# Native-unit softmax normalisation and the first layer's w_out low parts: which engine does them

## The chip, the cores and the metric

The kernel runs on one core of one Trainium2 chip. The metric is the time of one execution on the device in microseconds (us); what is compared is the median of several runs. The core's engines work side by side, each through its own instruction queue in a fixed order: TensorE (PE in the profile; PEld is its weight load), VectorE (DVE), ScalarE (ACT), GpSimd (POOL) and SyncE (SP, which issues DMAs here).

## What is computed

A causal attention with a forget bias, then two MLPs. Shapes: q, k, v are 4 x 8 x 576 x 64 (batch, heads, positions, head width); the MLPs take 2304 tokens of width 512 through 2048 hidden channels. The weights come as float64.

```
scores = where(causal, -1e9, scale * q @ k.T + min(bias, 0))
attn = exp(scores - max(scores))
attn = attn / (sum(attn) + 1e-9)
x = (attn @ v), heads side by side: 2304 x 512
x = (s * max(x @ moe_w_in, 0) ** 2 + b) @ moe_w_out
h = x @ moe2_w_in
out = (max(h, 0) + alpha * min(h, 0)) @ moe2_w_out
```

## The kernel before

**Attention in units.** A unit is one batch, one range of query rows (rows 0 to 319 in three blocks, or rows 320 to 575 in two) and one pair of heads: 32 units in all. The first eight, all of batch 0, are called *native*: their matmuls run on plain float32. The first four of these run before any MLP work. The other 24 split each operand into a high and a low float32r part.

**A head of a unit** (`scores`, then `values`) goes through the engines like this. The bias goes into a tile `probs` (VectorE L435 for head 0, ScalarE L431 for head 1), GpSimd masks its diagonal (L439), TensorE makes the scores (L457), VectorE adds both and takes the running maximum (L461), ScalarE takes the exponential and its row sum (L473). VectorE adds 1e-9 and takes the reciprocal of the sums (L480, L481), the blocks are multiplied by it (L484), TensorE transposes them (L515), a copy brings them out of PSUM (L519, ScalarE or VectorE) and TensorE multiplies them by v (L531). A block is 64 x 64, 128 x 192 or 128 x 320 elements in the first range, 128 x 448 or 128 x 576 in the second.

**Weights in packets.** The first layer's 16 packets each hold a w_in and a w_out tile of 128 x 512. Each tile is loaded as float64, made into float32 by three instructions (`convert`: ScalarE L140, VectorE L141 and L142) and then split: ScalarE casts the high part (L130), and the low part is the difference of the tile and its high part (L131, helper `split`). All 16 packets are made while the native units run.

**MLP blocks.** A block is 256 tokens; at each of 16 steps it takes one packet up (L783) and down (L897). Its hidden tile is split too, in the first layer by ScalarE (`gh`) and GpSimd (`gl`, L131). The first MLP block needs units 0 to 3; the next ones need later units, which are interleaved with the running block.

**The order.** The code gives a program order, and a scheduler lays out each engine's queue from it. At the start of attention, dummy matmuls (L97) are placed at fixed points among the first four units' work.

Of the kernel before, what the change touches and what calls it, by code (L numbers as in the profile page):

```python
# [12 lines left out]
AF = mybir.ActivationFunctionType  # L13
ALU = mybir.AluOpType
# [5 lines left out]
def tile_forget_attention__then__two_mlps(  # L20
# [20 lines left out]
    nc = tc.nc  # L41
# [52 lines left out]
    def busy(n):  # L94

        for _ in range(n):
            tc.keep_in_program_order(nc.tensor.matmul(scratch, dense[:, :P], dense, start=True, stop=True))  # L97
# [31 lines left out]
    def split(hi, lo, src, lo_eng=nc.vector):  # L129
        nc.scalar.copy(hi, src)  # L130
        lo_eng.tensor_tensor(out=lo, in0=src, in1=hi.bitcast(F32), op=ALU.subtract)  # L131
# [14 lines left out]
    def slot(n, dtype, name):  # L146
        return wp.tile([P, 512], dtype, tag=f"w{n}", name=name)
# [27 lines left out]
    def weight_tiles(f):  # L175

        if f not in SPARE:
            return [slot(n, F32R, f"w1_{f}_{n}") for n in SPLIT[SLOT[f]]]
        tiles = []
        for tag, pool, cols, n in SPARE[f]:  # L180
            t = pool.tile([P, cols], F32R, tag=tag, name=f"w1_{f}_{len(tiles)}")
            tiles += [t[:, i * 512 : (i + 1) * 512] for i in range(n)]
            if f == 0:
                rests.append(t[:, 512 : 512 + 2 * P])
        return tiles
# [3 lines left out]
    def fetch(layer, f):  # L189
        if (layer, f) in fetched:  # L190
            return fetched[layer, f]
        w_in, w_out = ((w_in1, w_out1), (w_in2, w_out2))[layer]


        def raw(name, n):
            if layer == 1:
                if f % 2:
                    tile_ = one.tile([P, 1024], U32, tag=("xh0", "xl0")[n], name=name)
                else:
                    tile_ = two.tile([P, 1088], U32, tag="probs", name=name)  # L200
            else:
                pool, tag = RAW[2 * f + n]
                tile_ = pool.tile([P, 20 * D if tag == "vs" else 1024], U32, tag=tag, name=name)
            return tile_[:, :1024].rearrange("p (n z) -> p n z", z=2)

        wi = raw(f"wi{layer}_{f}", 0)
        wo = raw(f"wo{layer}_{f}", 1)
        nc.sync.dma_start(
            out=wi.rearrange("p (c n) z -> p c (n z)", c=NCC),
            in_=w_in[:, f * 2 * P : (f + 1) * 2 * P].rearrange("(c p) n -> p c n", p=P),  # L210
        )
        nc.sync.dma_start(out=wo.rearrange("p n z -> p (n z)"), in_=w_out[f * P : (f + 1) * P, :])
        fetched[layer, f] = wi, wo
        return wi, wo

    def load_packet(layer, f):
        wi, wo = fetch(layer, f)
        t = weight_tiles(f) if layer == 1 else []
        values_ = []
        for n, src in enumerate((wi, wo)):  # L220
            if layer == 1:
                pool, tag, cols = WT[(2 * f + n) % len(WT)]
                wt = pool.tile([P, cols], U32, tag=tag, name=f"wt{f}_{n}")[:, :512]
            elif (f, n) == (NF - 1, 1):
                wt = two.tile([P, 512], U32, tag="ph", name="last")
            else:
                wt = slot(WHOLE[f][n], U32, f"wt0_{f}_{n}")
            convert(src, wt)
            values_.append(wt.bitcast(F32))
        for n, wt in enumerate(values_):  # L230
            if layer == 0:
                t += [slot(m, F32R, f"w0_{f}_{len(t)}_{m}") for m in SPLIT[f][2 * n : 2 * n + 2]]
            split(t[2 * n], t[2 * n + 1], wt, nc.gpsimd if layer == 0 and n else nc.vector)
        return [x.rearrange("p (c n) -> p c n", c=NCC) for x in t[:2]] + t[2:]


# [167 lines left out]
    def scores(u, h):  # L404

        own = HALF[h]
        head = u.b * H + u.h0 + h
        flip = u.native and h == 1
        nr = len(u.blocks)
        nm = two.tile([P, 3], F32, tag="nm", name=f"nm_{u.tag}_{h}")  # L410
        sm = two.tile([P, 3], F32, tag="sm", name=f"sm_{u.tag}_{h}")
        if u.rng == 0:
            nc.gpsimd.memset(sm[:, 0:1], 1.0)
        big = None if u.early else two.tile([P, 1088], F32, tag="probs", name=f"probs_{u.tag}_{h}")
        probs, col = {}, 0
        for r in u.blocks:
            i0, i1 = IB[r]
            rows = i1 - i0
            if u.early and r != 1:
                big, col = u.buf(two, 0, F32, "", f"probs{h}{r}"), 0  # L420

            width = -(-i1 // P) * P if i1 < S else S
            pt = probs[r] = big[:, col : col + width]
            col += width
            if width > i1:
                nc.gpsimd.memset(pt[:, i1:], 0.0)
            if r == 0:
                nc.gpsimd.memset(pt[64:P, 0:64], 0.0)

            if flip:  # L430
                nc.scalar.activation(  # L431
                    pt[:rows, :i1], u.cums[h][:rows, :i1], AF.Relu, scale=-1.0, bias=cumT[:rows, r, head : head + 1]
                )
            else:
                nc.vector.tensor_scalar(  # L435
                    out=pt[:rows, :i1], in0=u.cums[h][:rows, :i1], scalar1=cumT[:rows, r, head : head + 1],
                    scalar2=0.0, op0=ALU.subtract, op1=ALU.min,
                )
            nc.gpsimd.affine_select(  # L439
                out=pt[:rows, i0:i1], in_=pt[:rows, i0:i1], pattern=[[-1, rows]], base=0,  # L440
                channel_multiplier=1, compare_op=ALU.is_ge,
                fill=-MASKED if flip else MASKED,
            )
        u.probs[h] = probs
        for m, r in enumerate(u.blocks):
            i0, i1 = IB[r]
            rows, n = i1 - i0, i1
            a0 = i0 - u.q0
            pt = probs[r]
            init = -KEEP_ALL if flip else KEEP_ALL  # L450
            for j0, j1 in ([(0, n)] if n <= 512 else [(0, 320), (320, n)]):
                sc = u.bank("sc", f"sc{h}_{r}_{j0}")

                scr, all_ = sc[:rows, : j1 - j0], sc[:, : j1 - j0]
                aq = slice(a0, a0 + P)
                if u.native:
                    nc.tensor.matmul(all_, u.qk[0][own, aq], u.qk[1][own, j0:j1], start=True, stop=True)  # L457
                else:
                    nc.tensor.matmul(all_, u.xs[h][0][:, aq], u.xs[h][1][:, j0:j1], start=True, stop=False)
                    nc.tensor.matmul(all_, u.ql[h][:, aq], u.xs[h][1][:, j0:j1], start=False, stop=True)  # L460
                nc.vector.tensor_tensor_reduce(  # L461
                    out=pt[:rows, j0:j1], in0=scr, in1=pt[:rows, j0:j1], scale=SCALE if flip else -SCALE, scalar=init,
                    op0=ALU.subtract if flip else ALU.add, op1=ALU.max if flip else ALU.min,
                    accum_out=nm[:rows, m : m + 1],
                )
                if u.n < EARLY:
                    busy(1)
                init = nm[:rows, m : m + 1]
            if flip:
                nc.vector.tensor_scalar(  # L470
                    out=nm[:rows, m : m + 1], in0=nm[:rows, m : m + 1], scalar1=-1.0, scalar2=None, op0=ALU.mult
                )
            nc.scalar.activation(  # L473
                pt[:rows, :n], pt[:rows, :n], AF.Exp, bias=nm[:rows, m : m + 1], scale=1.0 if flip else -1.0,
                accum_out=sm[:rows, m : m + 1],
            )
            yield
        if u.n == 0:
            busy(4)
        nc.vector.tensor_scalar(out=sm[:, :nr], in0=sm[:, :nr], scalar1=1e-9, scalar2=None, op0=ALU.add)  # L480
        nc.vector.reciprocal(sm[:, :nr], sm[:, :nr])  # L481
        for m, r in enumerate(u.blocks):
            rows, n = IB[r][1] - IB[r][0], IB[r][1]
            nc.gpsimd.tensor_scalar(  # L484
                out=probs[r][:rows, :n], in0=probs[r][:rows, :n], scalar1=sm[:rows, m : m + 1],
                scalar2=1.0, op0=ALU.mult, op1=ALU.mult,
            )
        yield

    def values(u, h):  # L490
# [465 lines left out]
    def packet(layer, f):  # L956
        if (layer, f) not in packets:
            packets[layer, f] = load_packet(layer, f)
        return packets[layer, f]
# [92 lines left out]
```

## Time and profile before

| | us |
|---|---|
| runs shown: median (lowest to highest) | 1039.78 (1039.27 to 1041.05) |
| profiled execution, its own time | 1040.97 |
| span from its first to its last instruction | 1039.2 |
| TensorE busy in the span | 1019.4 |
| VectorE, ScalarE, GpSimd busy | 681.3, 672.4, 457.6 |

The profiled execution took 1.77 us beside its span and 1.19 us more than the median. TensorE's busy time is a union of overlapping matmuls whose ends are modelled, so a busy TensorE can still be waiting now and then. Shares over the whole span hide that the first 135 us differ from the rest: attention of the native units and the making of the packets lie there.

### The profile page before, as it was taken

Reading aid. Unit: us, or ns where it says so; the run is one execution under the profiler, and the core shown is the slowest. Engines: PE = TensorE matmul, PEld = TensorE weight load, DVE = VectorE, ACT = ScalarE, POOL = GpSimd, SP = SyncE. Lnnn points to the kernel's source line nnn. Section 1 sums busy time; section 2 is a strip of 40 time slices with the busy share of each in tenths; the row PEclk is TensorE's granted clock in tenths of the full one; section 3 lists DMA queues with packets and bytes.
Section 4 is the critical chain, followed back from the end, with each engine's and each line's share of the span. In section 5 each row is a group of like instructions: output and inputs, shape, how many; then the busy total and the mean of one; then the engine's idle time right before and its main releaser. Section 6 shows DMA issues by size and latency. Waiting matters only on the chain. (4 is left out here: it accounts for less than half of the span.)

```text
span 1039.2 us, 20636 instructions
## 1 busy us (share of the span) xinstructions
PE 1019.4 (98%) x6952; PEld 925.8 (89%) x6952; DVE 681.3 (66%) x1605; ACT 672.4 (65%) x1669; POOL 457.6 (44%) x876
## 2 busy tenths in 40 slices
PE   9899999999999999999999999999999999999997
PEld 4568899999999999999999888888899999999996
DVE  6979865787676776677655865857665456455443
ACT  5877876777787877778776776645454455445433
POOL 5656775666677666777562000574611011001000
PEclk9999999999999999999999999999999999999999
DMA  7988433343232432334215762645644335334331
GB/s 167 255 211 239 132 68 70 71 93 79 40 92 64 102 72 52 79 68 91 66 35 173 240 192 74 207 147 170 196 163 142 103 112 172 103 99 136 104 104 46
DMA packets 197930, 125.45 MB, mean 121 GB/s; under 512 B 138496, under 2 KB 167936, under 8 KB 197824
## 3 DMA queue, kind: packets, MB, share of 16 engines
q1 hardware_dynamic: 193744, 123.56, 42.8%
q8 instruction: 55, 0.90, 0.4%
q10 hardware_dynamic: 4080, 0.57, 0.3%
q14 instruction: 51, 0.42, 0.1%
HBM read 106.19 MB, written 17.90 MB: 119 GB/s over the span
## 5 line engine op out<-in xcount | busy, mean ns | idle before, releaser
L783 PE MATMUL hp<-xh,w 128*128 128x256 f32 (+1 forms) x1024 | 229.0, 300 | 0.3 <-ACT r L802 0.3
L907 PE MATMUL acc<-w,ring 128*128 128x512 f32 x864 | 214.6, 392 | 1.1 <-DVE ring L131 0.7
L907 PEld LDWEIGHTS acc<-w,ring 128*128 128x128 f32 x864 | 155.8, 188 | 29.3 <-DVE ring L131 1.1
L783 PEld LDWEIGHTS hp<-xh,w 128*128 128x128 f32 x1024 | 171.4, 189 | 6.2 <-ACT r L802 0.5
L897 PE MATMUL acc<-gh,w 128*128 128x256 f32 x896 | 172.4, 286 | 0.5 <-ACT res L926 0.5
L783 PE MATMUL hp<-xl,w 128*128 128x256 f32 (+1 forms) x512 | 152.6, 298 | 0.0
L897 PEld LDWEIGHTS acc<-gh,w 128*128 128x128 f32 x896 | 136.0, 189 | 3.2 <-issue 1.6
L883 POOL TENSOR_TENSOR cc<-u,t 128x256 f32<-128x256 f32 x32 | 26.1, 817 | 235.5 <-DVE u L874 201.5
L897 PE MATMUL acc<-gl,w 128*128 128x256 f32 x448 | 118.7, 288 | 2.2 <-POOL gl L131 2.2
L484 POOL TENSOR_SCALAR probs<-probs,sm 64x64 f32<-64x64 f32 (+4 forms) x160 | 91.0, 581 | 60.5 <-DVE sm L481 49.9
L473 ACT ACTIVATE probs<-probs,nm 64x64 f32<-64x64 f32 (+4 forms) x160 | 90.0, 563 | 38.5 <-DVE nm L461 32.7
L131 POOL TENSOR_TENSOR gl<-r,gh 128x256 fp32r<-128x256 f32 x112 | 89.5, 799 | 48.6 <-ACT gh L130 42.1
L817 PE MATMUL p<-xs,sums 128*128 128x256 f32 x768 | 104.7, 282 | 0.4 <-DVE u L859 0.4
L783 PEld LDWEIGHTS hp<-xl,w 128*128 128x128 f32 x512 | 97.1, 190 | 3.3 <-issue 0.4
L817 PEld LDWEIGHTS p<-xs,sums 128*128 128x128 f32 x768 | 98.0, 189 | 2.1 <-DVE u L859 0.6
L461 DVE CUSTOM_DVE_ANT_0 probs<-sc,probs 128x320 f32<-128x320 f32 (+3 forms) x160 | 68.2, 427 | 41.2 <-PE sc L460 32.8
L817 PEld LDWEIGHTS p<-xs,w 128*128 128x128 f32 x576 | 79.0, 189 | 8.7 <-DVE u L874 2.0
L802 ACT ACTIVATE r<-hp 128x256 f32<-128x256 f32 (+1 forms) x144 | 58.0, 403 | 44.1 <-PE hp L783 33.2
L817 PE MATMUL p<-xs,w 128*128 128x256 f32 x576 | 82.3, 282 | 2.4 <-DVE u L874 1.5
L897 PEld LDWEIGHTS acc<-gl,w 128*128 128x128 f32 x448 | 80.1, 188 | 5.0 <-POOL gl L131 2.8
L828 DVE SCALAR_TENSOR_TENSOR ph<-pl,misc,ph 128x512 f32<-128x512 f32 x64 | 51.7, 807 | 42.4 <-ACT pl L844 42.4
L515 PE MATMUL pt<-ident,probs 128*128 128x128 f32 x480 | 74.3, 275 | 4.6 <-POOL probs L484 4.4
(149 smaller groups left out, 2116.8 us busy)
## 6 DMA issues: line engine op xcount, KB each, us to landing
sums<-sums_d SPq DMA_DIRECT2D x128, 256.0 KB, 2.7
wi<-in_moe_w_in_dram SPq DMA_DIRECT2D x32, 512.0 KB, 4.7
wo<-in_moe_w_out_dram SPq DMA_DIRECT2D x32, 512.0 KB, 4.8
cum<-cum_d SPq DMA_DIRECT2D x32, 288.0 KB, 3.7
sums_d<-w SPq DMA_DIRECT2D x64, 128.0 KB, 1.8
cum<-cum_d SPq DMA_DIRECT2D x30, 160.0 KB, 3.0
nat<-in_k_dram SPq DMA_DIRECT2D x64, 72.0 KB, 2.5
x_d<-res SPq DMA_DIRECT2D x18, 256.0 KB, 2.2
```

What stands on the lines that cost most here:

```text
L131: lo_eng.tensor_tensor(out=lo, in0=src, in1=hi.bitcast(F32), op=ALU.subtract)
L461: nc.vector.tensor_tensor_reduce(out=pt[:rows, j0:j1], in0=scr, in1=pt[:rows, j0:j1], scale=SCALE if flip else -SCALE, scalar=init, op0=AL ...
L473: nc.scalar.activation(pt[:rows, :n], pt[:rows, :n], AF.Exp, bias=nm[:rows, m : m + 1], scale=1.0 if flip else -1.0, accum_out=sm[:rows, m ...
L484: nc.gpsimd.tensor_scalar(out=probs[r][:rows, :n], in0=probs[r][:rows, :n], scalar1=sm[:rows, m : m + 1], scalar2=1.0, op0=ALU.mult, op1=A ...
L515: nc.tensor.transpose(tp[:, o : o + P], u.probs[h][r][:, k0 : k0 + P], ident)
L783: nc.tensor.matmul(hs, a[:, c], b[c], start=(n == 0), stop=(n == len(terms) * NCC - 1))
L802: relus.append(nc.scalar.activation(r, hs, AF.Relu, scale=1.0 / W_SCALE).ins)
L817: nc.tensor.matmul(bank, lhs[:, c * P : (c + 1) * P], rhs[:, c], start=(start and c == 0 and z == 0), stop=(c == 1 and z == 2), skip_group ...
L828: nc.vector.scalar_tensor_tensor(out=r, in0=u, scalar=nalpha[:, f : f + 1], in1=r, op0=ALU.mult, op1=ALU.add).ins
L883: nc.gpsimd.tensor_tensor(out=cc[:, T:], in0=u3, in1=t5, op=ALU.add)
L897: nc.tensor.matmul(banks[d] if count == 2 else acc[d // 2][:, d % 2], a[:, d * P : (d + 1) * P], b, start=(f == 0 and (d % 2 == 0 or count ...
L907: nc.tensor.matmul(banks[m], a[:, m * P : (m + 1) * P], b, start=(f == 0 and b is woh and a is gh), stop=(f == NF - 1 and a is gl),)
```

## The change

Two pieces of work leave GpSimd. The 20 multiplications of head 0 of the eight native units (4 units with 3 blocks, 4 with 2) go to ScalarE, as a Copy with a scale per row; the 20 of head 1 go to VectorE. The 24 other units keep GpSimd. And the low parts of the first layer's 16 w_out tiles go from GpSimd to VectorE, which makes those of w_in already. From the line of the edit on, line numbers of the changed kernel are 3 to 6 higher.

```diff
@@ load_packet
-            split(t[2 * n], t[2 * n + 1], wt, nc.gpsimd if layer == 0 and n else nc.vector)
+            split(t[2 * n], t[2 * n + 1], wt, nc.vector)
@@ scores
         for m, r in enumerate(u.blocks):
             rows, n = IB[r][1] - IB[r][0], IB[r][1]
-            nc.gpsimd.tensor_scalar(
-                out=probs[r][:rows, :n], in0=probs[r][:rows, :n], scalar1=sm[:rows, m : m + 1],
-                scalar2=1.0, op0=ALU.mult, op1=ALU.mult,
-            )
+            pt, by = probs[r][:rows, :n], sm[:rows, m : m + 1]
+            if not u.native:
+                nc.gpsimd.tensor_scalar(out=pt, in0=pt, scalar1=by, scalar2=1.0, op0=ALU.mult, op1=ALU.mult)
+            elif h:
+                nc.vector.tensor_scalar(out=pt, in0=pt, scalar1=by, scalar2=None, op0=ALU.mult)
+            else:
+                nc.scalar.activation(pt, pt, AF.Copy, scale=by)
         yield
```

The scheduler lays the queues out anew. The first place is VectorE's queue at head 1 of the first unit, before (-) and now (+). Here `sm` holds the sums, `probs_0_0_1_333` is the head's tile, and `wt_0_0_196` the first weight tile.

```order
 L481 RECIPROCAL sm_0_0_1_331<-sm_0_0_1_331 128x3
 L470 TENSOR_SCALAR nm_1_0_1_442<-nm_1_0_1_442 64x1
-L461 ISA probs_0_1_0_445,nm_1_0_1_442<-sc_1_0_0_1_0_478,probs_0_1_0_445 128x192
-L461 ISA nm_1_0_1_442 128x1
+L470 TENSOR_SCALAR nm_1_0_1_442<-nm_1_0_1_442 128x1
+L488 TENSOR_SCALAR probs_0_0_1_333<-probs_0_0_1_333,sm_0_0_1_331 64x64
+L488 TENSOR_SCALAR probs_0_0_1_333<-probs_0_0_1_333,sm_0_0_1_331 128x192
+L488 TENSOR_SCALAR probs_0_0_1_333<-probs_0_0_1_333,sm_0_0_1_331 128x320
+L375 STREAM_TRANSPOSE turnedq_3_0_377<-natq_3_0_179 128x320
+L141 TENSOR_SCALAR wt_0_0_196<-wt_0_0_196 128x512
+L375 STREAM_TRANSPOSE turnedk_3_0_378<-natk_3_0_180 128x320
 L480 TENSOR_SCALAR sm_1_0_0_382<-sm_1_0_0_382 128x3
```

The three multiplications now stand right behind the reciprocal, and the first weight tile's conversion (L141) stands behind them.

The second place is GpSimd's queue between the units 2 and 4; first before, where `w0_1_2`, `w0_2_2` and `w0_3_2` are low parts of w_out tiles of packets 1 to 3:

```order
L131 TENSOR_TENSOR w0_1_2_5_239<-wt0_1_1_230,w0_1_2_6_238 128x512
L484 TENSOR_SCALAR probs10_0_2_0_585<-probs10_0_2_0_585,sm_0_2_0_1_583 64x64
L484 TENSOR_SCALAR probs10_0_2_0_585<-probs10_0_2_0_585,sm_0_2_0_1_583 128x192
L484 TENSOR_SCALAR probs12_0_2_0_597<-probs12_0_2_0_597,sm_0_2_0_1_583 128x320
L413 MEMSET sm_0_3_0_1_723 128x1
L484 TENSOR_SCALAR probs00_0_3_0_664<-probs00_0_3_0_664,sm_0_3_0_0_662 64x64
L131 TENSOR_TENSOR w0_2_2_9_259<-wt0_2_1_250,w0_2_2_10_258 128x512
L484 TENSOR_SCALAR probs00_0_3_0_664<-probs00_0_3_0_664,sm_0_3_0_0_662 128x192
L484 TENSOR_SCALAR probs02_0_3_0_676<-probs02_0_3_0_676,sm_0_3_0_0_662 128x320
L131 TENSOR_TENSOR w0_3_2_13_658<-wt0_3_1_649,w0_3_2_14_657 128x512
```

And now:

```order
L413 MEMSET sm_0_2_0_1_583 128x1
L413 MEMSET sm_0_3_0_0_662 128x1
L439 AFFINE_SELECT probs_0_0_1_0_817<-probs_0_0_1_0_817 128x128 x2
L439 AFFINE_SELECT probs_0_0_1_1_923<-probs_0_0_1_1_923 128x128 x2
L413 MEMSET sm_0_3_0_1_723 128x1
L426 MEMSET probs_0_1_1_0_987 128x64
L439 AFFINE_SELECT probs_0_1_1_0_987<-probs_0_1_1_0_987 128x128 x2
L131 TENSOR_TENSOR gl0_0_0_895<-r0_0_896,gh0_0_0_894 128x256
```

Only masks, small memsets and then the low parts `gl` of the first MLP block are left there.

The third place is TensorE's queue at the transposes (`pt0_0_0_1_1`) of head 0 of unit 5; `hp0_0_n` is the up step n of the first MLP block. First before:

```order
L897 MATMUL acc0_0_1_880<-gh0_0_1_1179,w0_1_2_5_239 128x256
L515 MATMUL pt0_0_0_1_1_1062<-ident_85,probs_0_1_1_0_987 128x128
L457 MATMUL sc1_4_0_0_1_1_1069<-turned_0_1_1_863 128x320
L457 MATMUL sc1_4_320_0_1_1_1072<-turned_0_1_1_863 128x256
L515 MATMUL pt0_0_0_1_1_1062<-ident_85,probs_0_1_1_0_987 128x128 x3
L515 MATMUL pt0_1_0_1_1_1079<-ident_85,probs_0_1_1_0_987 128x128 x5
L783 MATMUL hp0_0_3_1258<-xh0_0_869,w0_3_0_12_653 128x256
```

And now:

```order
L900 MATMUL acc0_0_1_880<-gl0_0_3_1272,w0_3_2_14_657 128x256
L518 MATMUL pt0_0_0_1_1_1062<-ident_85,probs_0_1_1_0_987 128x128
L457 MATMUL sc1_4_0_0_1_1_1069<-turned_0_1_1_863 128x320
L457 MATMUL sc1_4_320_0_1_1_1072<-turned_0_1_1_863 128x256
L518 MATMUL pt0_0_0_1_1_1062<-ident_85,probs_0_1_1_0_987 128x128 x3
L518 MATMUL pt0_1_0_1_1_1079<-ident_85,probs_0_1_1_0_987 128x128 x5
L786 MATMUL hp0_0_6_1536<-xh0_0_869,w0_6_0_24_1234 128x256
```

The MLP's up steps 3 to 5, the rest of its down step 1 and its down steps 2 and 3 now stand ahead of these transposes. From unit 9 on the two orders of TensorE differ only by a few swapped neighbours, and beyond the first third of each queue all of them read alike.

## Rows read from the trace of the kernel before

**Rows 1.** Busy time in four stretches; counts, clock, DMA share.

```profile
core 0: us, PE busy (x) PEld busy (x) DVE busy (x) ACT busy (x) POOL busy (x), PEclk, DMA share, GB/s
0.00:62.00 62.00, 55.52 (x227) 30.85 (x228) 48.27 (x159) 40.91 (x116) 35.95 (x112) 0.94 0.87 213
29.50:50.00 20.50, 18.59 (x82) 11.61 (x83) 19.53 (x68) 19.30 (x56) 10.98 (x24) 0.92 0.94 238
62.00:135.00 73.00, 71.80 (x473) 60.73 (x472) 65.81 (x133) 59.56 (x142) 48.52 (x70) 1.00 0.69 181
300.00:400.00 100.00, 100.00 (x837) 99.79 (x836) 71.34 (x209) 78.98 (x212) 68.15 (x143) 1.00 0.33 76
```

**Rows 2.** Waits of TensorE's weight loads, 0 to 62 us: total, times, longest.

```profile
PEld pt L515 <- POOL probs L484: 6.4, 8, 3.2
```

**Rows 3.** GpSimd's groups, 0 to 130 us: busy, mean ns, idle before.

```profile
L484 POOL TENSOR_SCALAR probs<-probs,sm 64x64 f32<-64x64 f32 (+4 forms) x38 | 24.0, 644 | 21.6 <-DVE sm L481 11.7 <-ACT xf L546 5.3 <-DVE nm L470 4.5
L131 POOL TENSOR_TENSOR w<-wt,w 128x512 fp32r<-128x512 f32 x15 | 19.9, 1328 | 9.7 <-ACT w L130 4.9 <-DVE w L131 3.2 <-ACT wt L140 1.5
```

**Rows 4.** VectorE's weight groups, forms apart, 0 to 140 us.

```profile
L141 DVE TENSOR_SCALAR wt<-wt 128x512 uint32<-128x512 uint32 x31 | 20.2, 656 | 3.3 <-ACT wt L140 3.1
L142 DVE SCALAR_TENSOR_TENSOR wt<-wi,wt 128x512 uint32<-128x512 uint32 x16 | 16.0, 997 | 0.2
L142 DVE SCALAR_TENSOR_TENSOR wt<-wo,wt 128x512 uint32<-128x512 uint32 x15 | 12.3, 821 | 0.1
```

**Rows 5.** Single lines, 0 to 140 us: ns min/median/max.

```profile
L141 DVE TENSOR_SCALAR wt<-wt x31: 385/506/1582, 19.5 to 124.3; 128x512 uint32<-128x512 uint32 x31
L142 DVE SCALAR_TENSOR_TENSOR wt<-wi,wt x16: 673/852/1776, 19.9 to 124.7; 128x512 uint32<-128x512 uint32 x16
L142 DVE SCALAR_TENSOR_TENSOR wt<-wo,wt x15: 668/682/1652, 25.0 to 122.9; 128x512 uint32<-128x512 uint32 x15
L131 DVE TENSOR_TENSOR w<-wt,w x16: 644/682/1242, 25.6 to 127.6; 128x512 fp32r<-128x512 f32 x16
```

**Rows 6.** VectorE in order of time: start us, us.

```profile
44.40 1.65 DVE L142 SCALAR_TENSOR_TENSOR wt<-wo,wt 128x512 uint32<-128x512 uint32 x1
...
49.37 1.88 DVE L435 TENSOR_SCALAR probs<-cum,cumT 128x448 f32<-128x448 f32 x2
```

**Rows 7.** GpSimd in order of time, beside these.

```profile
44.09 1.26 POOL L131 TENSOR_TENSOR w<-wt,w 128x512 fp32r<-128x512 f32 x1
45.34 1.70 POOL L484 TENSOR_SCALAR probs<-probs,sm 128x192 f32<-128x192 f32 x2
...
49.59 1.33 POOL L131 TENSOR_TENSOR w<-wt,w 128x512 fp32r<-128x512 f32 x1 [2.55 <-DVE w L131]
...
52.69 1.52 POOL L484 TENSOR_SCALAR probs<-probs,sm 64x64 f32<-64x64 f32 x3
```

**Rows 8.** VectorE's bias pair of a later unit, in order of time.

```profile
65.44 0.86 DVE L435 TENSOR_SCALAR probs<-cum,cumT 128x448 f32<-128x448 f32 x2
```

**Rows 9.** Bias groups of the native units, 0 to 130 us.

```profile
L431 ACT ACTIVATE probs<-cum,cumT 128x448 f32<-128x448 f32 (+4 forms) x17 | 8.8, 575 | 0.4 <-DMA cum<-cum_d 0.3
L435 DVE TENSOR_SCALAR probs<-cum,cumT 128x448 f32<-128x448 f32 (+4 forms) x17 | 11.2, 704 | 0.0
```

**Rows 10.** The end of unit 3's head 1: VectorE, then TensorE, in order of time.

```profile
52.36 0.16 DVE L481 RECIPROCAL sm<-sm 128x3 f32<-128x3 f32 x1
...
53.76 0.55 PE L515 MATMUL pt<-ident,probs 128*128 128x128 f32 x3 [2.79 <-POOL probs L484]
```

**Rows 11.** A wait of TensorE's weight loads, 62 to 135 us.

```profile
PEld acc L897 <- POOL gl L131: 1.0, 1, 1.0
```

**Rows 12.** First up matmul; then the sixth w_in low part and the sixth step's matmul.

```profile
61.67 0.47 PE L783 MATMUL hp<-xh,w 128*128 128x256 f32 x1
...
69.23 0.69 DVE L131 TENSOR_TENSOR w<-wt,w 128x512 fp32r<-128x512 f32 x1
...
92.18 0.36 PE L783 MATMUL hp<-xh,w 128*128 128x256 f32 x1
```

## Prediction

> **What bounds the kernel now.** I read the busy time by stretch first [rows 1]. Late in the span, at 300 to 400 us, TensorE is busy for 100.00 of 100 us and its weight loads for 99.79: it is fed without a gap, and nothing that GpSimd, VectorE or ScalarE do earlier or later there can show. In the first 62 us, until the first MLP block begins (61.67 us, [rows 12]), its weight loads are busy for 30.85 us alone: this stage waits, and here time can be won or lost. From 62 to 135 us, where the other four native units and eleven packets of weights are made beside the first MLP block, weight loads reach 60.73 of 73 us: nearly full, with little to win.
>
> Next, who makes the first stage wait. In 29.5 to 50 us VectorE is busy for 19.53 of 20.5 us and ScalarE for 19.30: both are full at once, GpSimd (10.98) is not. But GpSimd is waited for all the same: TensorE's transposes wait 6.4 us in 8 waits for the multiplication on GpSimd [rows 2]. At 53.76 us one sees such a wait: 2.79 us of TensorE idle, ended by GpSimd's three multiplications [rows 10]; the reciprocal began at 52.36, GpSimd at 52.69, and it needs 1.52 us for the set [rows 7].
>
> Third, VectorE's own durations, since it is full. L142 on 128 x 512 takes 673 ns at least but 997 in the mean on w_in tiles, and 668 against 821 on w_out tiles; L141 has 385 and 656 [rows 4, 5]. The long ones stand over GpSimd work: the 1.65 us at 44.40 over a low part that GpSimd began at 44.09 and a multiplication at 45.34, and the 1.88 us of a bias pair at 49.37 over a low part begun at 49.59, while a like pair takes 0.86 us elsewhere [rows 6 to 8]. So part of VectorE's busy time is waiting for GpSimd, and what leaves GpSimd gives some of it back.
>
> **What it costs VectorE.** Multiplications of eight heads: a bias pair on the same shapes takes 0.86 us [rows 8], from below 8 x 0.86 = 6.9 us; from above 20 x 704 ns = 14.1 us, the blocked mean of the bias group [rows 9]. I take 1.0 us a head, 8.0, nearer to the free pair because GpSimd will be emptier. Low parts: 16 x 0.68 us, the median of those that VectorE makes already [rows 5], 10.9 us (bounds 644 and 1242 ns: 10.3 and 19.9). Together 18.9 us. Four heads and five low parts fall into the first stage (7.4 us), four heads and ten low parts into the second (10.8).
>
> **What it gives back.** Mean less minimum, times count: L141 31 x 0.271 = 8.4 us, L142 16 x 0.324 + 15 x 0.153 = 7.5 [rows 4, 5], bias 17 x (0.704 - 0.43) = 4.7 [rows 8, 9]; 20.6 us at most. The leaving work is 24.0 + 19.9 = 43.9 us [rows 3] of GpSimd's 35.95 + 48.52 = 84.5 [rows 1], so by shares 10.7 us; both long cases shown lie over leaving work, so more. I take 13, bounds 5 and 20.6, half in each stage: VectorE's account is then 7.4 - 6.5 = +0.9 us in the first and 10.8 - 6.5 = +4.3 in the second.
>
> The Trainium skill (SBUF — State Buffer, "Who interferes with whom") says that VectorE and GpSimd share a port pair under an exclusive lock, held for the whole instruction, which VectorE wants in its two-port modes or with two SBUF inputs; by it L141, L142 and the bias all contend, the trace's long instructions agree, and VectorE's new low parts would themselves still meet the masks that GpSimd keeps. Another page (Perfetto Trace Analysis, "Optimizing Scalar/DVE Operations") warns that moving operations between these two might not help: by that, all that VectorE takes over and all that it gets back cancel, and the time stays at 1039.8. The rows make it 18.9 against 13.
>
> **ScalarE.** ScalarE's bias instructions have the same 20 shapes and a per-row operand: 575 ns in the mean [rows 9], 20 x 0.575 = 11.5 us; 14 of them (8.1 us) in the first stage, where ScalarE idles 62 - 40.91 = 21.1 us, but only 1.2 us while it is full [rows 1]. Nothing is given back to it in these rows. The six blocks of head 0 of units 2 and 3 fall in or near the full stretch; most of their 3.5 us can slide into the idle time around it, and I charge 1.0 us.
>
> **The chain.** A set of multiplications leaves a queue where it took 1.52 us and stood among low parts of 1.3 us [rows 7] for one of about 1.0 us. I take 0.5 us for each of the 8 waited sets, -4.0 us; bounds 0 (VectorE is as late as GpSimd was) and the 6.4 us waited. **First stage:** -4.0 + 0.9 + 1.0 = -2.1 us.
>
> **Second stage.** VectorE's +4.3 us meets 73 - 65.81 = 7.2 us of idle time. The weights have cover: the sixth packet's w_in low part is there at 69.92 us and its step's first matmul runs at 92.18 [rows 12], 22 us later. If that cover is gone, each low part costs its 0.68 us. The heads are what becomes late, and the new order puts MLP steps in front of them on TensorE. I take +0.5 us. GpSimd's `gl`, no longer behind low parts of 1.3 us, ends the wait of 1.0 us among the weight loads [rows 11]: -1.0 us. Stage: -0.5; the 16th low part, after 135 us, is lost among TensorE's work.
>
> **Sum.** -2.1 - 0.5 = -2.6 us: of the profiled execution 1040.97 us makes 1038.4. That execution is 1.19 us above the median, so on the scale of the runs it is 1039.78 - 2.6 = 1037.2 us. A measurement of this kernel tells about 0.2%, 2.1 us, from no change.
>
> **Rivals.** *VectorE becomes the bound; slower.* For it: it is full in 29.5 to 50 us and at 65.81 of 73 later, and in the new order three multiplications stand ahead of the first weight tile's conversion. If it gets back only 5 us, the first stage has 7.4 - 2.5 = +4.9, the second 10.8 - 2.5 - 7.2 = +1.1, and the multiplications queue as long as on GpSimd (no -4.0): about +5 with `gl`'s -1.0, 1045 us. With the chain's gain kept, it decides below about 8 us given back, where half of the missing 5 us eats the 2.6. Against it: the long instructions lie over work that leaves. Chance 0.23.
>
> *ScalarE takes what VectorE frees; no change.* It is as full as VectorE in 29.5 to 50 us. If all 3.5 us of the units 2 and 3 stay on the path, the first stage is +0.4 and the sum about 0: 1039.7. Against it: 21.1 us of idle time around. Chance 0.24.
>
> *All waits on GpSimd go; much faster.* TensorE's 6.4 us and `gl`'s 1.0 vanish and VectorE gets all back: -7.4, about 1032.4. Against it: the reciprocal itself is late, as at 52.36 us, because VectorE is full. Chance 0.15.
>
> The forecast itself, 1035.5 to 1039, has 0.38. The clock can shift each: a mean of 0.94 over 62 us [rows 1] is some 7 us at 1.2 GHz instead of 2.4, and if new gaps or a new order end or double that, TensorE gains or loses up to 3.5 us; that is inside the range.
>
> **Numbers.** Faster by over 0.2%: the last rival's 0.15 and most of the forecast (0.33), 0.48. Within: the ScalarE rival and the forecast's rest, 0.28. Slower: 0.24. The range leaves out about half of the much faster case and half of the slower one: 1032.5 to 1043.
>
> **What would show it.** Right: L141 and L142 nearer to their minima of 0.39 and 0.67 us in the mean; VectorE's busy time over 0 to 135 us up by about 5 us and not 19; no wait of TensorE for GpSimd's multiplication before unit 8; block 0's first up matmul about 2 us ahead of 61.7. Wrong: long VectorE instructions now over masks and `gl`; TensorE waiting for multiplications on VectorE or ScalarE as long as it did; a stage after 62 us that is longer than before.

## The result, and the profile after

The change makes the kernel slower: 1048.38 us in the median of 6 runs (1046.92 to 1052.61) for 1039.88 (6 runs, 1039.10 to 1041.05), a ratio of 1.0092 with a 95% interval of 1.0070 to 1.0115. The profiled execution took 1048.14 us with a span of 1046.4. That is 8.5 us more, where 2.6 us less were forecast.

First the busy times in the stretches of [rows 1], in the kernel after (two stretches are added):

```profile
core 0: us, PE busy (x) PEld busy (x) DVE busy (x) ACT busy (x) POOL busy (x), PEclk, DMA share, GB/s
0.00:62.00 62.00, 50.62 (x204) 28.44 (x204) 44.66 (x167) 42.62 (x122) 17.77 (x81) 0.92 0.89 210
29.50:50.00 20.50, 13.06 (x57) 7.87 (x55) 17.11 (x60) 19.05 (x53) 1.10 (x4) 0.92 0.98 247
62.00:135.00 73.00, 72.14 (x482) 61.37 (x480) 59.61 (x144) 61.69 (x145) 23.76 (x37) 1.00 0.64 174
135.00:160.00 25.00, 22.35 (x163) 20.54 (x162) 17.04 (x49) 16.65 (x47) 14.36 (x38) 1.00 0.34 67
300.00:400.00 100.00, 99.82 (x832) 99.41 (x831) 72.53 (x215) 80.28 (x219) 69.88 (x151) 1.00 0.37 83
```

Beside [rows 1] one sees that in 29.5 to 50 us, where VectorE and ScalarE were full, every engine is less busy now. VectorE is busy for 17.11 us where it was 19.53, ScalarE for 19.05 where it was 19.30, GpSimd for 1.10 where it was 10.98. TensorE lost all the same: its weight loads fell from 11.61 to 7.87 us there. Over the whole of the two stages ScalarE is the one of these three that became busier (42.62 us for 40.91, and 61.69 for 59.56). And TensorE now has gaps at 135 to 160 us: 22.35 of 25 us, where the same stretch of before's trace has 25.00.

What the moved work costs, and what it gives back, in the groups that answer to [rows 4, 9] (VectorE and ScalarE, 0 to 140 us; busy, mean ns of one, idle before):

```profile
L141 DVE TENSOR_SCALAR wt<-wt 128x512 uint32<-128x512 uint32 x31 | 13.1, 436 | 1.2 <-ACT wt L140 1.1
L142 DVE SCALAR_TENSOR_TENSOR wt<-wi,wt 128x512 uint32<-128x512 uint32 x16 | 11.6, 724 | 0.1
L142 DVE SCALAR_TENSOR_TENSOR wt<-wo,wt 128x512 uint32<-128x512 uint32 x15 | 10.8, 723 | 0.1
L131 DVE TENSOR_TENSOR w<-wt,w 128x512 fp32r<-128x512 f32 x31 | 23.1, 745 | 2.4 <-ACT w L130 2.2
L435 DVE TENSOR_SCALAR probs<-cum,cumT 128x448 f32<-128x448 f32 (+4 forms) x17 | 6.1, 390 | 0.4 <-DMA cum<-cum_d 0.4
L488 DVE TENSOR_SCALAR probs<-probs,sm 64x64 f32<-64x64 f32 (+4 forms) x18 | 6.0, 381 | 0.1
L490 ACT ACTIVATE probs<-probs,sm 64x64 f32<-64x64 f32 (+4 forms) x20 | 9.9, 553 | 0.0
```

The multiplications cost what was charged or less (381 ns on VectorE, 553 on ScalarE), the low parts a little more (745 ns for 680). L141 fell from 656 to 436 ns in the mean, L142 on w_in tiles from 997 to 724, the bias from 704 to 390.

Where the time went: the waits of TensorE, in 0 to 62 us and then in 143 to 180 us (total, times, longest). Here `pt` is the transposed block in PSUM and `pf` its copy; `av` and `acc_first` are its products with v; `hp` is the result of an up step and `r` its activation:

```profile
PE pt L518 <- DVE probs L488: 5.6, 1, 5.6
PE acc_first L534 <- ACT pf L522: 3.5, 1, 3.5
...
PE hp L786 <- ACT r L805: 1.8, 2, 1.4
PE acc L900 <- ACT w L130: 1.5, 1, 1.5
PE pt L518 <- POOL probs L486: 0.6, 1, 0.6
```

There are two places. In the first, the wait for GpSimd of [rows 2, 10] is gone, but one wait of 5.6 us for a multiplication on VectorE and one of 3.5 us for a copy on ScalarE stand there instead. VectorE's instructions ahead of the 5.6 us, in order of time, and TensorE behind them:

```profile
44.93 0.15 DVE L480 TENSOR_SCALAR sm<-sm 128x3 f32<-128x3 f32 x1
46.88 1.04 DVE L375 STREAM_TRANSPOSE turned<-nat 128x832 f32<-128x832 f32 x1 [1.80 <-DMA cum<-cum_d]
...
48.25 0.68 DVE L142 SCALAR_TENSOR_TENSOR wt<-wi,wt 128x512 uint32<-128x512 uint32 x1
48.85 0.87 DVE L435 TENSOR_SCALAR probs<-cum,cumT 128x448 f32<-128x448 f32 x2
49.64 0.16 DVE L481 RECIPROCAL sm<-sm 128x3 f32<-128x3 f32 x1
...
50.84 1.05 DVE L488 TENSOR_SCALAR probs<-probs,sm 64x64 f32<-64x64 f32 x3
...
51.63 1.51 PE L518 MATMUL pt<-ident,probs 128*128 128x128 f32 x6 [5.59 <-DVE probs L488]
```

The sums of unit 2's head 1 are ready at 44.93 us. But between them and their reciprocal, VectorE's new queue has a transpose for unit 4, which waits 1.80 us for a DMA, then score steps of unit 3, a step of a weight's conversion and a bias pair; more weight work stands behind the reciprocal. The multiplication runs 5.9 us after the sum. In before's trace the sum ran at 39.76 us, the reciprocal at 40.63, and GpSimd began at 40.90. By the Trainium skill (PSUM — Partial Sum Buffer, "Engine vs sequencer instructions") the queues of ScalarE, VectorE and GpSimd are strictly first in, first out; the rows agree, since nothing passes the transpose while it waits.

The first up matmul of the MLP, to be read beside the one of [rows 12] (61.67 us):

```profile
64.95 0.47 PE L786 MATMUL hp<-xh,w 128*128 128x256 f32 x1
```

It is 3.3 us late. From the starts of the up matmuls in both traces, counted in their order, I worked out how the lag goes on: +3.3 us at 62 us, then -6.3 at 109 us (the MLP's steps stand ahead of the heads in the new queue), +9.6 at 187 us, when the late heads come through, and +8.3 us from 220 us on without change to the last of them at 688 us; the span ends 7.2 us later (1046.4 for 1039.2). So the loss is made before 220 us, some 3 us of it in the first place and some 5 in the second, around 150 to 170 us.

### The profile page after: what moved, and what is told of

Its sections match the earlier page's. It is cut to its first block, busy times and chain, and to the rows that moved or that the text cites. A ratio compares the mean times of both kernels' runs of the same rounds, so it can differ in the third digit from the quotient of the medians.

```text
span 1046.4 us, 20622 instructions
## 1 busy us (share of the span) xinstructions
PE 1019.2 (97%) x6952; PEld 927.0 (89%) x6952; DVE 677.3 (65%) x1641; ACT 681.1 (65%) x1689; POOL 416.1 (40%) x820
## 5 line engine op out<-in xcount | busy, mean ns | idle before, releaser
L786 PE MATMUL hp<-xh,w 128*128 128x256 f32 (+1 forms) x1024 | 229.2, 301 | 1.8 <-ACT r L805 1.8
L786 PEld LDWEIGHTS hp<-xh,w 128*128 128x128 f32 x1024 | 171.5, 190 | 8.3 <-ACT r L805 2.1
L900 PE MATMUL acc<-gh,w 128*128 128x256 f32 x896 | 170.2, 286 | 2.0 <-ACT w L130 1.5
L786 PE MATMUL hp<-xl,w 128*128 128x256 f32 (+1 forms) x512 | 152.3, 298 | 0.0
L131 POOL TENSOR_TENSOR gl<-r,gh 128x256 fp32r<-128x256 f32 x112 | 92.3, 825 | 62.8 <-ACT gh L130 51.7
L786 PEld LDWEIGHTS hp<-xl,w 128*128 128x128 f32 x512 | 97.1, 190 | 2.7
L486 POOL TENSOR_SCALAR probs<-probs,sm 128x448 f32<-128x448 f32 (+3 forms) x120 | 66.2, 565 | 38.7 <-DVE sm L481 38.0
```

What stands on the lines that cost most here:

```text
L486: nc.gpsimd.tensor_scalar(out=pt, in0=pt, scalar1=by, scalar2=1.0, op0=ALU.mult, op1=ALU.mult)
L786: nc.tensor.matmul(hs, a[:, c], b[c], start=(n == 0), stop=(n == len(terms) * NCC - 1))
L900: nc.tensor.matmul(banks[d] if count == 2 else acc[d // 2][:, d % 2], a[:, d * P : (d + 1) * P], b, start=(f == 0 and (d % 2 == 0 or count ...
```

## The experiments

**Theory A:** the loss comes from the order into which the scheduler laid the queues. **Theory B:** VectorE and ScalarE can't take the work, in any order. To tell them apart I fixed every queue to a written order. The programs of before and after hold the same instructions in the same program order and differ only in the engine of 56 of them, so an order of one can be used for the other. The lines below stand at the end of the kernel's body; `QUEUES` holds numbers of traced instructions, per engine:

```diff
+    traced = list(nc.cur_bb.bb.instructions)
+    behind = mybir.DependencyInfo(mybir.DependencyClass.NoSync, mybir.DependencyReason.DATA)
+    for text in QUEUES.values():
+        queue = [traced[k] for k in read_queue(text)]
+        for a, b in zip(queue, queue[1:]):
+            tc.add_manual_dep(b, a.name, behind, reason="queue")
```

In the runs e1 and e2 the table stands ahead of the code, so their lines are 288 and 287 higher than those of after and before. Ratios are to the kernel before on the same chip (medians 1039.98 to 1041.05 us).

**e1: the work moved, the queues of before.** A moved multiplication stands behind its reciprocal, a low part where its input was ready.

> The full change (multiplications of the first eight units on ScalarE and VectorE, w_out lo parts on VectorE), but every engine's queue is pinned to the order that it had before the change; a moved instruction is put into its new engine's queue at the place where its input was ready in the trace of before. Theory A (the loss comes from the order into which the scheduler laid the queues after the change): no loss is left, 1030 to 1040 us, since the load terms that the trace after confirmed (bit operations near their minima, VectorE's busy time lower) remain. Theory B (VectorE and ScalarE take the moved work at a cost, in any order): still 1045 to 1051 us.

1040.09 us; ratio 1.0001 (0.9983 to 1.0018). That is 0.1 us above theory A's bounds and 5 us below theory B's. Nothing is lost, and fixing the queues shows no cost here; but nothing is gained. The place of [rows 10] in this trace, VectorE and then TensorE:

```profile
51.40 0.16 DVE L769 RECIPROCAL sm<-sm 128x3 f32<-128x3 f32 x1
51.60 0.84 DVE L776 TENSOR_SCALAR probs<-probs,sm 64x64 f32<-64x64 f32 x3
52.36 0.68 DVE L419 TENSOR_TENSOR w<-wt,w 128x512 fp32r<-128x512 f32 x1
52.97 0.21 DVE L810 COPY pf<-pt 128x64 f32<-128x64 f32 x1
...
53.32 0.87 PE L806 MATMUL pt<-ident,probs 128*128 128x128 f32 x3 [2.90 <-DVE pf L810]
...
61.96 0.47 PE L1074 MATMUL hp<-xh,w 128*128 128x256 f32 x1
```

The transposes start 0.44 us earlier than in [rows 10] (53.76), close to the 0.5 us that the prediction took for a set. But the wait, 2.90 us, is as long as the one it replaced: now VectorE's copy out of PSUM ends it, behind a low part. Both stand there in the trace of before too, which ran that copy at nearly the same time:

```profile
53.05 0.21 DVE L519 COPY pf<-pt 128x64 f32<-128x64 f32 x1
```

It ended at 53.26 us, 0.50 us before the transposes started. The copy would have held them until then in any case, so this set could win no more than 0.50 us, however fast it became. The first up matmul is not earlier (61.96 for 61.67).

**e2: the work of before, the queues of after.**

> The work stays on the engines of before (all 56 instructions on GpSimd), but every queue is pinned to the order of the kernel after; the 56 stand in GpSimd's queue where VectorE or ScalarE ran them in the trace after. Theory A: the loss shows without any work moved, 1045 us or more (GpSimd is slower at the work, so it can be more than the 1048 of the full change). Theory B: 1038 to 1042 us, as before.

1053.55 us; ratio 1.0130 (1.0107 to 1.0152). With no work moved, the new order alone costs 13 us. That is more than the whole change costs: GpSimd has the work here at places that were laid out for other engines, and TensorE's longest waits are for it:

```profile
PE pt L802 <- POOL probs L771: 7.0, 3, 4.2
```

Theory B falls with these two runs: in the new order the move even helps (ratio 1.0092 for 1.0130), in the old one it changes nothing.

**e3, e4: the parts alone, queues laid out by the scheduler.** Only the low parts, or only the multiplications; e4 is after with

```diff
-            split(t[2 * n], t[2 * n + 1], wt, nc.vector)
+            split(t[2 * n], t[2 * n + 1], wt, nc.gpsimd if layer == 0 and n else nc.vector)
```

and e3 is before with the same line the other way round.

> Only the 16 w_out lo parts go to VectorE; the scheduler lays out the queues itself. Theory A: the time depends on the order that comes out, which is a third one (its TensorE queue stands further from both kernels than these from each other), so anything from 1034 to 1050, and the trace's TensorE gaps must name waits behind other work in a queue. Theory B: 16 of the 36 added instructions on VectorE cost their share, 1042 to 1045.

> Only the 40 multiplications move (20 to ScalarE, 20 to VectorE); the w_out lo parts stay on GpSimd; the scheduler lays out the queues itself. Theory A: depends on the order, 1034 to 1050, with gaps of TensorE behind other work in a queue. Theory B: most of the loss, 1043 to 1047.

e3: 1041.04 us, 1.0015 (0.9996 to 1.0035). e4: 1050.92 us, 1.0103 (1.0083 to 1.0123). The loss comes with the multiplications, though not in the same order: in e4 TensorE waits 5.3 us for a multiplication on ScalarE and 2.8 us for one on VectorE in the first 62 us. Theory B's bounds miss both times (e3 lies 1.0 us below them, e4 3.9 us above). Theory A's hold e3 and miss e4 by 0.9 us, but they were so wide (1034 to 1050 us) that this says little.

**e5, e6: one place each.** The instructions that before had started by 61.7 us in one order, those that follow in the other.

> The full change with pinned queues, cut in two at the first MLP matmul: the instructions that before had started by 61.7 us stand in the order of the kernel after, all that follow in the order of before. Theory A by the gaps of TensorE: the first place alone costs 3.3 us (first MLP matmul at 65.0 for 61.7), so 1042 to 1045 us. If the loss were one of the second place alone: 1039 to 1041.

> The full change with pinned queues, cut the other way: the instructions of the first 61.7 us in the order of before, all that follow in the order of the kernel after. Theory A by the gaps of TensorE: the second place (150 to 170 us, some 5 us of gaps more) is there, the first is not, 1043 to 1046 us. If the second place's gaps are only a consequence of the late first MLP matmul: 1039 to 1041.

e5: 1046.24 us, 1.0054 (1.0029 to 1.0078), above its bound of 1045. e6: 1045.33 us, 1.0047 (1.0028 to 1.0066). Each place costs about half, and the second is no consequence of the first: in e6 the first up matmul runs at 61.79 us, and TensorE's longest waits at 143 to 180 us are for the same two tiles as after's:

```profile
PE hp L786 <- ACT r L805: 1.4, 2, 1.1
PE acc L900 <- ACT w L130: 1.4, 1, 1.4
```

**e7: two moves in the queues of after.** VectorE's reciprocal and multiplications of unit 2's head 1 go behind their sum; ScalarE's `pf` copy goes 7 instructions forward. VectorE's part:

```diff
 L480 sm_0_2_0_1
+L481 sm_0_2_0_1
+L488 probs10_0_2_0, probs10_0_2_0, probs12_0_2_0
 L375 turned_0_0_1
...
-L481 sm_0_2_0_1
...
-L488 probs10_0_2_0, probs10_0_2_0, probs12_0_2_0
```

> The full change with its own queues pinned, and two moves in them: on VectorE the reciprocal of unit 2's second head and its three multiplications stand right behind their sum, ahead of the transpose that waits 1.80 us for a DMA; on ScalarE the copy of one pf tile stands 7 instructions earlier, behind the cast that was running when its input was there. Theory A: the waits of TensorE for these two (5.6 and 3.5 us) go and the first MLP matmul comes at 60 to 63 us, so 1043 to 1046 us (the second place stays). If the waits only hide a late VectorE (theory B), other waits take their place and it stays at 1047 to 1050.

1052.98 us; 1.0111 (1.0081 to 1.0141), above the bounds of both theories. Both waits went, but others came. The two longest waits of TensorE in 0 to 62 us, then three stretches with their clock (the last column but two):

```profile
PE av L534 <- ACT pf L522: 7.4, 2, 5.2
PE pt L518 <- ACT probs L490: 1.9, 1, 1.9
...
38.00:48.00 10.00, 8.59 (x24) 4.77 (x24) 7.36 (x27) 9.19 (x26) 0.10 (x1) 0.51 1.05 238
50.00:58.00 8.00, 2.83 (x13) 1.66 (x12) 6.35 (x22) 5.58 (x16) 4.26 (x5) 0.82 1.02 253
58.00:70.00 12.00, 12.00 (x32) 7.39 (x31) 4.51 (x19) 5.23 (x15) 0.00 (x0) 0.50 0.39 126
```

TensorE ran at 1.2 GHz in 38 to 48 us, with a pause of 1.91 us before 39.41 us, and again in 58 to 70, behind one of 5.17 us. In after's trace these two stretches are at 2.4 GHz (1.00).

**e8: queues of before, only head 0's multiplications moved (to ScalarE).** VectorE gets nothing. The edit to after, beside the low parts on GpSimd again and the order:

```diff
-            if not u.native:
+            if not u.native or h:
                 nc.gpsimd.tensor_scalar(out=pt, in0=pt, scalar1=by, scalar2=1.0, op0=ALU.mult, op1=ALU.mult)
```

> All queues pinned to the order of before, only the 20 multiplications of head 0 move, to ScalarE; VectorE gets nothing. The run with the whole change in the old order gained nothing, with VectorE busy 36 to 54 us without a break. Theory A1 (VectorE is full there, so the relief of the lock is spent on the 36 added instructions): without added work on VectorE the relief is a gain, 1036 to 1039 us. Rival A2 (the chain through exponentials, clock and transposes sets that stretch): 1039.5 to 1041.

1040.50 us; 0.9998 (0.9982 to 1.0013). Theory A1 falls and A2's bounds hold: even where VectorE is relieved and takes no new work, nothing is gained.

**e9 to e12: a better order of one stretch.** In the queues of before, at 44 to 64 us, 38 instructions of VectorE and 24 of ScalarE are put so that the chain of units 3 and 4 comes first and weights that are needed later follow; with the work moved (e9) and not moved (e10). In e11 and e12 one cast of ScalarE goes further back as well.

> The full change in the old queues, with one stretch of two queues rearranged (38 instructions of VectorE and 24 of ScalarE, 44 to 64 us): unit 3's sums, normalisation and pf copies and unit 4's chain stand first, the conversions of the weight packets 2 to 4 behind them. Theory A (the place in the queue decides, and VectorE is full there because weights that are needed later run first): TensorE's wait of 2.9 us ahead of unit 3's second transposes and part of the next go, the first MLP matmul comes at 57 to 60 us for 62.0, so 1035 to 1038.5 us. Rival (the chain through the exponentials and the clock sets the stretch, or the weights come late after it): 1039 to 1042.

> The same rearranged stretch with the work on the engines of before (GpSimd's queue has the masks and multiplications of units 3 and 4 ahead of its lo parts there). Theory A: most of the gain is the order's and comes without the move, 1036 to 1039.5 us; if it is the move that pays once the order is right, 1039.5 to 1042 here and 2 us or more above the run with the work moved.

e9: 1042.61 us, 1.0022 (1.0008 to 1.0037); e10: 1044.14 us, 1.0031 (1.0013 to 1.0048). Both lie above every bound that I gave. In e9 the wait of 2.9 us went, and my own order made a new one: ScalarE's cast waited for VectorE with the exponentials behind it, and TensorE behind these.

```profile
56.91 0.62 ACT L130 CAST w<-wt 128x512 fp32r<-128x512 f32 x1 [2.88 <-DVE wt L142]
...
61.99 0.47 PE L518 MATMUL pt<-ident,probs 128*128 128x128 f32 x1 [2.95 <-ACT probs L490]
```

> As the run of the full change with the weights later, but without the new wait that the trace of that run showed: on ScalarE the cast of packet 3's w_out, which held unit 4's exponentials for 2.88 us while it waited for VectorE, stands behind them and behind unit 4's normalisation. Theory A: the wait of 2.95 us ahead of unit 4's transposes shrinks to 1 us or less and the first MLP matmul comes at 57 to 60.5 us, 1035 to 1039 us. Rival C (each wait that is moved leaves a pause of TensorE elsewhere in this stage, and a pause lowers the granted clock behind it, so single moves don't pay): 1039.5 to 1043.

> The same queues with the work on the engines of before. Theory A: the order pays in either placement, 1036 to 1040 us, and within 1.5 us of the run with the work moved. If the move itself pays in the better order: 2 us or more above it. Rival C: 1040 to 1045.

e11: 1041.69 us, 1.0010 (0.9997 to 1.0022); e12: 1039.83 us, 0.9998 (0.9985 to 1.0011). No gain in either placement. e11 lies inside rival C's bounds. e12 lies inside theory A's (0.2 us below C's), but A's claim was that the order pays, and its interval holds 1; it is also 1.9 us below e11, so the move itself does not pay in the better order.

**e13 to e18: the pauses filled.** Over the 340 executions listed in the results, within each kernel, 0.01 less of mean granted clock goes with 7.9 us more; the mean is 0.990 for after, 0.995 for before. **Theory D:** a pause costs its length and then the lower clock. The idle matmuls of L97 are put into pauses, by hand in TensorE's queue (the lines of e13, e14, e17 and e18 are 4 to 6 higher than after's, L792 for L786). `fill`, of which only the definition is shown, is called ahead of a head's transposes and of its products with v, and `FILL` says how many matmuls go to which place:

```diff
+    def fill(where):
+        for _ in range(FILL.get(where, 0)):
+            nc.tensor.matmul(scratch, dense[:, :P], dense, start=True, stop=True)
```

> The full change with its own queues, pinned, and 35 more of the kernel's idle matmuls on TensorE (of a tile of zeros, into a bank that nobody reads): 13 in the pause of 3.5 us at 30 to 33.6 us, 22 in that of 5.6 us at 46 to 51.6 us. The waits stay, only the clock behind them should. Theory D (a pause costs its length and then the lower clock behind it; mean clock 0.990 for 0.995 of before, and 7.7 us for each 0.01 over all executions): mean clock 0.993 to 0.996 and 1043 to 1046 us. If the clock is only a symptom: 1047 to 1050.

> The full change in the old queues, with 10 more idle matmuls in the pause of 2.9 us at 50.4 to 53.3 us. Theory D: the clock does not fall behind that pause (3.5 us at 1.2 GHz in that trace), mean clock 0.997 or more, 1036.5 to 1039 us. If the clock is only a symptom: 1039.5 to 1041.

> The kernel before with its own queues, pinned, and 10 more idle matmuls in its pause of 2.8 us at 51 to 53.8 us. Theory D: one of its two stretches of 3.4 us at 1.2 GHz goes, mean clock 0.996 to 0.998, 1037 to 1039.5 us. If the clock is only a symptom: 1039.8 to 1041.

> As the run before it, with 3 idle matmuls more ahead of unit 2's first transposes (35.7 us in the trace of before, a wait of 0.56 us, behind which the clock fell at 37.4 us). Theory D: both stretches at 1.2 GHz go, mean clock 0.998 or more, 1035.5 to 1038.5 us. If it is not that wait that lowers the clock there: the time of the run with 10.

> The full change in the old queues with 10 idle matmuls in the pause at 50.4 to 53.3 us and 8 in the one at 39.8 to 42.0 us, behind which the clock fell in the run with 10 alone. Theory D: mean clock 0.997 or more and 1037 to 1039.5 us. If the clock then falls behind another pause: as the run with 10, 1039.5 to 1041.

> The full change; the first 61.7 us in the order of the kernel after with the 35 idle matmuls in its two pauses, what follows in the order of before. Theory D with two places: both losses are off, 1038.5 to 1042 us (1046.2 without the idle matmuls, 1046.1 with them but with the new order behind). If the new order of the first place costs more than its pauses' clock: 1043 to 1046.

| run | us | ratio (95%) | mean clock |
|---|---|---|---|
| e13 | 1046.08 | 1.0048 (1.0028 to 1.0068) | 0.996 |
| e14 | 1040.40 | 0.9986 (0.9966 to 1.0006) | 0.995 |
| e15 | 1040.37 | 1.0000 (0.9983 to 1.0017) | 0.996 |
| e16 | 1041.03 | 1.0000 (0.9983 to 1.0017) | 0.995 |
| e17 | 1040.02 | 0.9995 (0.9976 to 1.0015) | 0.998 |
| e18 | 1044.56 | 1.0042 (1.0027 to 1.0057) | 0.997 |

The matmuls do hold the clock. The pause of e1 and the 4 us behind it, without them (e1) and with 10 of them (e14):

```profile
50.00:54.00 4.00, 1.10 (x6) 0.73 (x6) 3.96 (x13) 3.09 (x8) 1.49 (x4) 0.68 1.00 354
54.00:58.00 4.00, 4.00 (x13) 2.58 (x13) 1.88 (x8) 3.07 (x8) 0.00 (x0) 0.50 1.08 241
...
50.00:54.00 4.00, 4.00 (x20) 2.25 (x19) 3.79 (x14) 3.14 (x8) 1.39 (x3) 1.00 0.99 339
54.00:58.00 4.00, 4.00 (x20) 2.34 (x18) 2.48 (x10) 3.06 (x8) 0.00 (x0) 1.00 1.14 262
```

What the clock gives back in time is less clear. Each kernel is compared with before on its own chip. e13 lies 0.0044 below after (1.0048 for 1.0092), some 4.6 us, and 0.006 of mean clock would be 4.7 by the line above; the two intervals leave about 3 us to either side of that. e18 lies 0.0012 below e5, 1.2 us, where 0.008 would be 6.4. For the old queues it is nothing that can be measured: from e1 to e17 0.0006, where 0.004 would be 3.2 us. Of the bounds, e13 is 0.1 us above D's; e14 and e15 lie where the clock is only a symptom; e16 is 2.5 us above D's, and 0.7 us from e15; e17 has the clock that D asks for and is 0.5 us above D's time; e18 lies inside those for an order that costs more than its pauses' clock.

The first up matmul in the profiled executions of e13, e18 and e17, to be read beside 61.67 us in [rows 12]:

```profile
61.27 0.47 PE L792 MATMUL hp<-xh,w 128*128 128x256 f32 x1
...
64.16 0.39 PE L792 MATMUL hp<-xh,w 128*128 128x256 f32 x1
...
58.92 0.47 PE L792 MATMUL hp<-xh,w 128*128 128x256 f32 x1
```

e13's is ahead of before's, so there the first place costs nothing, and what is lost (3.4 us from 220 us on) comes from the second; but this execution, 1043.30 us at a clock of 1.000, is the fastest of its twelve. In e18's, at its median, the first place still costs 2.5 us. e17's lead of 2.8 us shrinks to 2.0 us at 187 us and 1.1 at the end. So D can hold for a part of the loss at most: e13 and e18 have a higher mean clock than before (0.996 and 0.997 for 0.995) and are still slower by more than their intervals. How far the line through the executions shows the price of a low clock, and how far only that the same pauses cost both, stays open. No run beats the kernel before; e14 comes nearest, and its interval holds 1.

## Why the prediction was wrong

**The load account was about right, and on the careful side.** *What it costs VectorE:* 0.381 us a multiplication makes 7.6 us for 20 (8.0 taken), 0.745 us a low part 11.9 us for 16 (10.9 taken). *What it gives back:* 31 x 0.220 for L141, 16 x 0.273 and 15 x 0.098 for L142, 17 x 0.314 for the bias, 18.0 us in all (13 taken, bounds 5 and 20.6). VectorE's busy time from 0 to 135 us is 104.27 us for 114.08; part of this is work that now comes after 135 us (310 instructions for 292, where 36 were added). In the old order (e1) nearly all of it is there, 326 instructions, and takes 110.30 us: 3.8 us less than before, where the prediction had about 5 us more. *ScalarE:* 20 x 0.553 = 11.1 us for 11.5. The Trainium skill's lock of VectorE's port (SBUF — State Buffer, "Who interferes with whom") fits: with GpSimd at 41.5 us for 84.5 most of the long instructions are gone (the longest L141 takes 0.56 us for 1.58). That it is this lock was not tested by itself. Its other page (Perfetto Trace Analysis, "Optimizing Scalar/DVE Operations") warned that such a move might not help, which is the result in the old order (1.0001), though not because load and relief cancel: VectorE was relieved on balance, and no time came of it.

**The step that failed first** is *the chain*: "I take 0.5 us for each of the 8 waited sets, -4.0 us". It priced how long a set takes once its engine begins, and left the queue around it as it was. At the one place that I had read, the size held (0.44 us in e1), and yet no time came of it, since the next wait in line, for VectorE's copy, took its place. I had put all of that idle time down to GpSimd; the copy at 53.05 us bounded the gain there at 0.50 us. In the kernel as built, a set waits for its turn: 5.9 us from sum to multiplication. So for -4.0 us the runs show no gain in the old order (e1), and +5.6 us for the first place of the new order (e5, 0.0054).

**The second** is *the heads*: "The heads are what becomes late, and the new order puts MLP steps in front of them on TensorE. I take +0.5 us." The size was wrong: +4.9 us (e6, 0.0047), paid at 143 to 170 us, behind the stage that I had looked at. The heads did become late. The last multiplications of a native unit, on GpSimd before and on VectorE after:

```profile
135.29 1.37 POOL L484 TENSOR_SCALAR probs<-probs,sm 128x448 f32<-128x448 f32 x2 [0.33 <-DVE sm L481]
...
144.33 0.89 DVE L488 TENSOR_SCALAR probs<-probs,sm 128x448 f32<-128x448 f32 x2
```

But of the waits of TensorE in 143 to 180 us only 0.6 us and 0.2 us are for a head's own tiles; 1.8 us are for `r` of the MLP block, and 1.5 us for the cast of the 16th packet's w_out tile, here before and after:

```profile
142.17 0.61 ACT L130 CAST w<-last 128x512 fp32r<-128x512 f32 x1
...
152.43 0.62 ACT L130 CAST w<-last 128x512 fp32r<-128x512 f32 x1 [0.56 <-DVE last L142]
```

Before, nothing waited for it. So the cover of 22 us that the prediction read at the sixth packet does not hold for the last one in the new order. That the late heads hold `r` and this tile up, standing ahead of them in their queues, was not tested.

**The rivals.** None of the three was this. The first, VectorE as the bound, came nearest with 1045 us; its sum leaves out the forecast's own +1.0 us for ScalarE and +0.5 for the heads, with which it is 1046.3. In 29.5 to 50 us neither VectorE nor ScalarE became fuller, and the waits for GpSimd's multiplications did go. One of the prediction's signs of being wrong came: TensorE waits 5.6 us for one set of multiplications on VectorE, where its weight loads had waited 6.4 us in eight waits for GpSimd's. The bounds of the range were made of loads and waits in the old queues; the order itself, of which the text ahead of the prediction shows three places, had no term of its own, and e1 and e2 show that it decides: 1040.1 us with the old order, 1053.6 without any work moved.

**What stays open:** how much of the first place's 5.6 us is the waits and how much the clock behind them, why the lead of the first stage in e17 does not last, and why each order other than the old one, mine as well, made its own pause. That the scheduler's choice follows from the costs that it assumes was not tried.

## What to carry to other kernels

Where a scheduler lays out the queues, moving an instruction to another engine is two changes, the load and the order. Time them apart: the new work in the old order and the old work in the new order are two runs, and they say more than any account of busy time. In a stage where several queues are nearly full, read for each wait what stands ahead of the instruction in its own queue, and what else the waiting instruction needs, since the next wait in line takes the place of the one removed.

## What had not been expected of the hardware

In e1 TensorE's granted clock was at 1.2 GHz behind a pause of 2.90 us, after work had come back: 0.50 in 54 to 58 us, with TensorE busy for 4.00 of 4 us. With ten matmuls on zeros in that pause (e14) it was 1.00. The time of one kernel varied with its clock: e5 ran from 1043.5 to 1053.0 us, with mean clocks of 0.993 to 0.983, where e17 (0.997 to 1.000) stayed within 1039.3 and 1042.3.
